# Projections of q and k and the kv tails as matmuls on half the rows, two at a time

## The chip, the cores and the metric

The kernel runs on one core of a Trainium2 chip. The metric is the device time of one execution in microseconds (us), as the median of several runs. A separate execution is recorded by the hardware profiler; its views are called the profile or the trace here. The engines are named as the profile names them: PE (TensorE, matmuls; PEld its weight loads), ACT (ScalarE), DVE (VectorE), POOL (GpSimd) and SP (SyncE, which only issues DMAs here).

## What is computed

Attention with a feature map, then a two-layer network with ELU on its output:

```python
# q, k, v: (8, 8, 576, 64) = batch, heads, rows, head_dim;  w_phi: (64, 128)
def phi(x):
    proj = np.einsum('bhsd,df->bhsf', x, w_phi)
    proj = proj - np.max(np.abs(proj), axis=-1, keepdims=True)
    return np.concatenate([np.exp(proj), np.exp(-proj)], axis=-1)
q_p, k_p = phi(q), phi(k)
kv  = np.einsum('bhsf,bhsd->bhfd', k_p, v)
z   = np.sum(k_p, axis=2)
num = np.einsum('bhsf,bhfd->bhsd', q_p, kv)
den = np.einsum('bhsf,bhf->bhs', q_p, z)[..., None] + 1e-06
x   = (num / den) as (batch * rows, heads * head_dim) = (4608, 512)
h   = x @ w_in                      # w_in (512, 2048)
g   = np.where(h > 0, h, np.exp(np.minimum(h, 0)) - 1)
out = g @ w_out                     # w_out (2048, 512), float32 (4608, 512)
```

## The kernel before

**Work.** The attention is done in 16 quads of four heads each (`plan_quad`, two quads per batch). A head has 576 rows: 512 in the main part and a tail of 64. The tails of two heads share 128 partitions. k and q come in as bf16 and are transposed, the first six quads on PE, the later ones by DMA from SP, into `kT` and `qT`, tiles of 128 partitions: two 64-wide row blocks lie one above the other, on partitions 0 to 63 and 64 to 127. The network (the MoE part of the names) is done in 9 chunks of 512 rows: one per batch from the main parts and one from all tails. A chunk has 16 steps of four matmuls (`mm1`, L975, into banks called `ph`), an exponential on ACT (L987), a subtraction on POOL (L991) and a maximum on DVE (L998), and then 4 x 4 steps of four matmuls (`mm2`, L1036, into `po`).

**The steps of a quad that the change touches.**

- `project` (L535) multiplies a 128-partition tile of `kT` or `qT`, as the stationary operand, with `w_phi_rhs` of 256 columns. That operand, `w_phi_both`, holds `w_phi` on the upper half of the partitions for the first 128 columns and on the lower half for the other 128, and zeros elsewhere, so that one matmul projects both row blocks, each against a half that is zero. Two such matmuls fill one PSUM bank `pk`; a quad has four such banks and a smaller one for the tails, for k and again for q.
- `reduce` (L546, DVE) takes the largest absolute value of each row from `pk` (`m_k`, `m_q`). For k, two exponentials per bank (L561, ACT; plus and minus sign) write `EK` and `EKt`.
- `features` (L668) projects q a second time with the features on the partitions: `w_phi_both[:, par, :]` is stationary and 512 columns of `qT` stream, one matmul into one bank `pq`. Two exponentials per bank (L691, ACT) write `Eq`; `tail_features` (L679) does the tails.
- `kv` (two steps, s = 0 and 1, each with a bank `pkv`): sixteen matmuls of 128 rows (L737) and then four on 64 rows for the tails (L749), s = 0 on partitions 0 to 63 and s = 1 on 64 to 127. `kv_copy` (L760, ACT or DVE) empties the bank.
- `outputs` (L794, `pn`) multiplies `Eq` with `kv`; `tail_outputs` (L809, `pnt`) does so for the tails, with 64 stationary columns, s = 0 on partitions 0 to 63 of the result and s = 1 on 64 to 127. `weigh` (L829) and `combine` (L835) on DVE, then a division, give `x`, which is transposed for the network.

**Order.** The program is written out in full, with each engine's instructions in a fixed order. That order comes from a planner that runs while the program is built (`Planner.run`): it plays the steps forward with a booked cost per step and engine, gives each free engine the ready step of the lowest rank (`RANKS`, one number per step, written into the file), and keeps account of the eight PSUM banks and of DMA: `MB_PER_US` and `MB_PER_US_OF_ONE` (rates), `LANDING` (time until a transfer is seen), `AHEAD` (how far POOL may issue loads in front). A step takes the banks in its list `new` all at once. Steps of the kind `first` (transposes, `pk`, `pq`) start only while they hold fewer than four banks, six before the network has begun:

```python
if kind == "first":
    if held[kind] >= (4 if moe[0] else 6):
        return False
if kind in ("first", "second"):
    n = held["first"] + held["second"] + len(o.new)
    if n > (6 if moe[0] else 8):
        return False
```

On the chip the engines follow the planned order and wait for semaphores; the booked costs are not used there.

Of the kernel before, what the change touches and what calls it, by code (L numbers as in the profile page):

```python
# [8 lines left out]
FP32 = mybir.dt.float32  # L9
# [25 lines left out]
    "0H2r0f2C0G0A2B0k1C0m0K2s092F0E0R201z082A3nD06f55H0Bn4v2+2eAL6C313+3d2o2x01120v2b"  # L35
    "00251m1c020x1Y1r212gBM2D0T173z2I0F1E0q8M07290uF42X2w3b0C0J3Y0h30262j2z1u472V1Z4P"
    "GR4E0LBl0O0o2u0S1x2q3p5F4-0Z150d0W4C28360n0a3c3I0Y4j6n1F4R9G2Q493q6r4L4W2y1T5B5J"
    "3T321g6I0U840s0r2h0z040w1n110i5s2W4x7l5l0B0-1A2n0+3E3x2J4D3J5+1b194n4h4H4m1B4a10"
    "3w7J8P4VAk51504f5A164s0y5D5q6t5N7Z1G1e3K6X4I401i1Q930j1W3h5G1f591v0X7p5O1R2R3v1s"
    "3r3l6R7s3A0cCh2L5x5e4e2vAY8IAZ23GQ7N4F3gGw7kHlDRAG3t4B433a7mH22dGk4r661w5C8BHg24"  # L40
    "Fd9T561hBb5iHC3QA37IAF2YDS9Z9-Av7+C3KX9jDG5n9zAU7FAACK2ZFZA48rBQ798dBLAN5RA89h9O"
    "5vC7AzCmFk9F4+BZDAJOHzA6BE184S3k5d4N4c1+335T7x0e6D0MCj4k1-695r1a1k5cAl715p6E860V"
    "5-7E6i2P6g6-4M0I570p6x2K6S6W3u0PGl7d5V2l746m7C6o8z7M5m7U3-3o6p7o7Q3y4y3O1D414G3P"
    "1o1S3D3m3V3S6L1l2-3C1X3G4Z1q2i3B680NAS5j8p9r5E5X3e6b6T7fAX5P0D7305606h4Y6KBP7X0t"
    "06Gs7A0g816v8e640QBG7T4QAc2H3H6c7W6l6U8f5Q6P7O726M9d7K3X5k8U5t7b8Y3f8G6N8Z7a6q9a"
    "82887D5z8W6e3N3W1U1J7i2f1I1O7r1M132M1H1L2E1V611t9k6B80899fC57z9KH32aDH8lHb9l8D67"
    "Me5W8754KxB0AfDcJtAH7h34C8AOBaAaF+AT9q9NA2CrOY9i9sF2GT2NHRKeGOAg482tBW5UBB2c8X8g"
    "AJAiOcC6Je6dCYAMK12pPBCAKU5KGrFKG5D5DW9JDqIjCXBwKdDbDXEQH+AQHK9mCPGXJ6IIJr9IJa6+"
    "70379M143i4z8t3L4w1y9L1jCa4XETHx7P7v03EVCG7L0lDCC98iBCD61p8aCkAwBg4K7jCz4639DK7B"
    "Bf1P9oDB8SBX6J9ULK9t0b5M7nGcA77S8A837u9D4iB1AKBcBH784JBoDF759x4O91588V4oAC984A2T"  # L50
    "3R8oAP429B4g8v8j766u8wBeHWCd539e92Ee5a9b9YCW6z4pE3JE6AB9K3Fw7q5uCNAxA5B5EqEBBSFI"
    "EXBr5I8-A9275h7V3U3Z5fB+ELDP4lF7BYCSCE355Z4bKyCV8y96CHAtEk8JDjBqC07Y907HCn957G5g"
    "855Y3j8c458hHeCc6G4TD3BA4UGJM48u8O9w2mC1CBJ1ENCoJb2OMSD1GzDNFn9PHBAjLxDTA1FrEvFy"
    "Jd2kFO94JcDyDUHOH8FvFP5yMEJAGiGU5oAnGqGEHGAeFTB6JxAqGmGMH7BDOiEfKT9yDOFcH1DlEKGb"
    "Bk9vDiG3HcDQPQOsBUG6I79QNiGZIJNcMOEwCyHVEHPxQ9JRG2IELTHLOxOBIM447t1K7g8x1ND97eAy"
    "9VCpEOEZFCARCQ7yCJ8KArB3BF9pBN9nBdCFBKAoDZAB628nE-D-DE8N22FM97EWDdBVCqFGEPDu6Y65"
    "Ct9gDYCxD+CwBIF8E2BsFpEFEa9X63HFBy9cAIDVDw5H9ECl5w7wCs4tEmBj8mSBFQ4qJ59HB-DJBpEu"
    "Au8F9SAD3MEME9BREcCME5B4D2G-BhGhHU7-D4BtFlIwESC2HYHj8s8C6FG43F6yDLD7E7EEE+BxG1CL"
    "Cu5LKwDzCiG0Kj9WE6B7E47RCRF-L8Fu8L6aE0I3F6AmDxAEH51dC-6QIQ6O4uJ79R778bFb4d8TAbA0"
    "6wEd9uJQAWAVGWLuKVEsLmJTH4DDPSC+LLD8H9FWDsFLCeHPJ8EzFtMHI8A+HfGvQ8K+GPIxS4FoNeIC"  # L60
    "VnF1LvONTLJ9F9EjS6BODmMyK2FVDeGGVwAsDkIZS2QaO0LhTRAhFiHiJMKkI+QtJVU5RfM2QkReEbK5"
    "HtK7JpJYJLLQInUNGKRBQJ6j8QGB522SGCElFAKAFqEyEGLPCUHrSjBvHyIrCCCg6HIWNMRXQDISC4BJ"
    "ECK4KlGFMUIGRoIVFxKpIPIkHvMFKbHaHDI6L5NlIFQEI1LyJuITNGHqIbPNIXGLI0M9LqFEDtKGCvDp"
    "CbIv6VJgM78kIf2U8+JXQBEDJfNaKJKFILIyJnFFDIKmMz7cMACIMmN1IuNLMdO7CfOpBzM-HQEIL7L4"
    "L0R7SWBT9+HZN0MRLtNXLlK-MDEYNZFmF0P4JNPIIADMIOJ4N6IaLiHNIqPPHsLdMWJBCZJjLkLoN9Ep"
    "DhJkGSEr3s99MV8q8EJP6sNvHh9AObJJ6kHXJqP9LXMqFsLwLGApMIN7SsJGJZDrV+EtFhIDTTEnGgM6"
    "SAAdFUEoW2JDLeLnQ-IzMgHmTbWyDvJyMLEiPHNFKaQpP-OUS3EgNrNTQ5J-GjKPP+K0GIKcUuWkDoDg"
    "Q6JKFgOrW9UIN+LJVBNWGNV5ToRRRaL-UtV4QHPjKqSJUaUCTFUPO9OJUUY6Tp8R5bEx2GKvHoIoFzJm"
    "HJGtMtRHEUIULBSIA-IYL1Q2KzGVLUB8PfI-JwMpKhKLLHNPPFPnPCHkLMEhIcMoKiIpOLMYQPKgP5Hw"
    "JlQGIsL2LVJvLFNVLcPDJiQ1IRKSMcL3G9DaIHG8KIMPItMiLOKOPUMQH6PRIgO-FBLNOjMhKQKYLCLz"  # L70
    "INLjIKLZF5LaN2HEJoJWN5I2BiMxLWHACTBuNKHIJ+MwB2Pg6ZKrNNK9NdQMMBHMO+KNN3OoOfOVFYMu"
    "I4PMKuJzEJJSM1LpKKLYNgHnPYPGPzOAO4KtLgNjLDNONIIhQ7OeHSPbJHP6M3NmE1KWKnOkQTIlLrMJ"
    "RKVkNDO1TSQrFJKEMKEAT7MNS8FDGdPhWAV8DnOEPcX4GHNfTmGAFSPWR+HTO2LsWNWsMkSkWWR0ODM+"
    "PvXrFjOOSgPpL+NkVpWnFRQfWeVLGaOmXyVXDfJIVuWhFaNnWMUqOKMrTzVdImVUVIRZVaX2VFVeUAPa"
    "WRWLUsW5WpXtUxV3VGYKUlBmJ2LRGoG+GDKCOGQRKHM8KfLEGnK6IiGYJCH-PtL6JFI5PsQIIeLbL9TE"
    "RpSQShNAYESYXvTMYAUFOXNbNpP8MfIdNQQ4SPU2KMMXO6SZXRI9GxPqXmSrOtCOLSKoNROhP7ThNYTG"
    "PuKDQ3Pi8HHdQKMGPkQUQNRQSbK8SqN4SFG7JsO5J3KBKsQsP0RFHpHuQONCRLRnF3LARvVYMjRVSnS-"
    "Q0MnN8NHSOUiRuTJGyR-S5TyGuPKRNQgT+NSJhRIJUP3TeR3RrRzOvOgERWaRxWXWbQVScRcUfS0RlNq"
    "U8QLPdVQSLSlO8QXSeSDMTUkT6PTRhWDPwTvUZSdSuUQQvOaJ0WxFNOPViPXMbT-VmXkGpUKQYWvOwNh"
    "WfY0HHLfTOUMNyOZYUP2RMRkX3WwMMV7WQRYOyUWWHQWTBV0YdX7U9UJVWUoMCNxVlQZGfVOWCQCFXSx"  # L80
    "XTQoNuOlWBPOOqXJVHTcUbXlUSXDTsXaXSY7U3W3XNVNTwYBU0S+XbWgXLYPTAE8PANBM0Y5RwR1KRQF"
    "SoSzRWWESyR6T3NUOSUrLIRDSUR8TYTnRJOnRGRjRqQxOWRmXoPJSRYLQQX-T2QhUGWSXOTqTgNEREMs"
    "QwRORsWPXpSwT1UeUTYJR4RTSmYNUOQiXIXCWIVhWFTVTjTWUVVqTxTuOQVSUHUcUERANJVTY4Y3PoVb"
    "PrUyRdTlUvWKQlW0S1SKSMSXVjXETUX+X9TtOTQST8SNR5SVTfQjVoTkWVU1XsRgTZT9YOU-RCStV2Wc"
    "U6V1TPSfYIV6WTSiSGUzVJSvSCUnW7VASSTdQzVfNoUjR2SaQAORRtQeR9VMPyOHUwSTPZMaWtSHUDTX"
    "Y9PeQmULWOWmXVSpXWP1OFUYYaPVTHSEVyQ+XeW4VxPlMvS9WuXzRPV-WrWiU4N-WJQyUgTNWYX0U7Qb"
    "S7QuXgT4YMW1OCUhW8UmKZOIVzY8O3WUWGXwOdRyYkRUX8OMYnWlNwX5TiTaXfYFTDXZWZXdXUYDYXXc"
    "VVVKX6XGUXXuXYXiYfXAYGNtVcW+UBVtYTY2FHV9WqWjURVDYWQqFeTCYVM5T5TQYmWoT0QdYYVsNzUp"
    "YgYHFfVrTrPLPEVCYZXBRbW-W6OuYQWdYRPmMlUdYbY1GeVEYeQnRSRiVvOzMZVPYiXxTKXXXhXKYcXq"
    "YSVRYjVZYlX1XMU+XjXQXnYCTIWzXFXPYhXHVg385S9CCDIBNsQc"  # L90
# [14 lines left out]
class Op:  # L105
    def __init__(self, cost, fn, deps, behind, new, uses, key, load, slot):
        self.cost = cost
        self.fn = fn

        self.deps = [d for d in deps if d is not None]  # L110
        self.behind = [d for d in behind if d is not None]
        self.new = new
        self.uses = uses
        self.key = key
        self.load = load
        self.slot = slot
        self.waits = 0
        self.then = []
        self.engine = None
        self.end = None  # L120
        self.seen = None


class Planner:
# [7 lines left out]
    MB_PER_US = 0.31  # L132
    MB_PER_US_OF_ONE = 0.26
    LANDING = 1.6
    AHEAD = 6.0
# [5 lines left out]
    def op(  # L141
        self, cost, fn, deps=(), behind=(), new=(), uses=(), key=0.0, load=None
    ):
        o = Op(cost, fn, deps, behind, list(new), list(uses), key, load, self.slot)
        for bank in o.new + o.uses:
            bank.users += 1
        self.ops.append(o)
        return o

    def run(self):  # L150
# [58 lines left out]
        while todo:  # L209
            started = False  # L210
            for e in ready:
# [35 lines left out]
                if o.load:  # L247
                    dma = max(dma, o.end) + o.load / self.MB_PER_US
                    o.seen = self.LANDING + max(
                        dma, o.end + o.load / self.MB_PER_US_OF_ONE  # L250
                    )
# [31 lines left out]
def kernel(  # L283
# [11 lines left out]
    P = 128  # L295
# [139 lines left out]
    def plan_quad(i):  # L435
# [38 lines left out]
        for n in range(2):  # L474
# [4 lines left out]
            if i >= DMA_QUAD:  # L479
# [6 lines left out]
                def tail_by_dma(e, n=n, t0=t0):  # L486
# [5 lines left out]
                    {"SP": 1.27}, by_dma, [main, *prior], key=-4.0, load=0.25  # L492
# [3 lines left out]
                    load=0.1,  # L496
# [35 lines left out]
        def project(n, hh, bank):  # L532
            pk = psum(bank, [P, 4, F], FP32, "pk")
            for j in range(2 if hh < 4 else 1):
                nc.tensor.matmul(  # L535
                    pk[:, 2 * j:2 * j + 2, :].rearrange("p a b -> p (a b)"),
                    in_tile(n)[:, 2 * hh + j, :],
                    w_phi_rhs,
                    start=True,
                    stop=True,  # L540
                )

        def reduce(n, hh, bank):
            o = (hh // 2) * NS + (hh % 2) * NT
            m = largest(n)
            nc.vector.tensor_reduce(  # L546
                m[:, o:o + NT] if hh < 4 else m[:, NS - 1::NS],
                bank.tile[:, 0:4 if hh < 4 else 2, :],
# [7 lines left out]
        for hh in range(5):  # L556
            bank = Bank("first")

            def exp_k(e, sg, hh=hh, bank=bank):
                n = 4 if hh < 4 else 2  # L560
                nc.scalar.activation(  # L561
                    EK()[:, hh, sg, :] if hh < 4 else EKt()[:, sg, :],
# [81 lines left out]
        for hh in range(5):  # L644
# [42 lines left out]
            def exp_q(e, sg, c=c, par=par, hh=hh, bank=bank):  # L687
                src = bank.tile
                if hh == 4:
                    src = src.rearrange("p a b -> p (a b)")  # L690
# [506 lines left out]
```

## Time and profile before

| | |
|---|---|
| median of 3 runs | 385.18 us (384.37 to 385.94) |
| the profiled execution's own time | 386.46 us |
| its span, first to last instruction | 384.7 us |
| granted PE clock, mean | 0.998 |
| MATMUL L1036 `po`, records | 550, mean 379 ns |
| MATMUL L975 `ph` from `xT`, records | 495, mean 379 ns |
| MATMUL L535 `pk`, records | 288, means 289 ns (k) and 274 ns (q) |
| MATMUL L668 `pq`, records | 61, mean 379 ns |
| ACT L561 `EK` and L691 `Eq` | 128 each, means 630 and 637 ns |
| DVE L546, k and q | 80 each, means 631 and 630 ns |

The profiled execution is one run, with a time of its own; the median is what is compared. A matmul's duration in the trace runs until its result is out, and the next one starts earlier: how long a row of matmuls takes is read from their starts. Some matmul records are missing. Shapes are given as rows*columns of the stationary operand, then partitions x columns of the streaming one.

### The profile page before, as it was taken

How to read it: one execution, taken by the hardware profiler on the slowest of the kernel's cores; microseconds unless marked ns; L12 is line 12 of the kernel's file. 1: busy time of each engine (PE TensorE's matmuls, PEld its weight loads, DVE VectorE, ACT ScalarE, POOL GpSimd, SP SyncE). 2: the span in 40 equal slices, each digit the busy share in tenths (PEclk: the TensorE clock that was granted, in tenths of full speed). 3: DMA queues.
4: the chain of work that ended last, by engine and by line, in shares of the span. 5: the costliest groups of instructions: out<-in, count | busy, mean ns of one | idle time of the engine just before them, and what ended most of it. 6: DMA issues, size and time to landing. Idle time of an engine off the chain costs nothing.

```text
span 384.7 us, 8031 instructions
## 1 busy us (share of the span) xinstructions
PE 360.1 (94%) x2932; PEld 201.9 (52%) x2978; DVE 265.1 (69%) x560; ACT 266.5 (69%) x576; POOL 245.9 (64%) x356
## 2 busy tenths in 40 slices
PE   3787899999999999999999999989999999999994
PEld 2466556655555545556665456545555554444442
DVE  2989799878677777799894679846963861747000
ACT  2999989677798589688687686677697523646111
POOL 9993999996783399279996642564377552737000
PEclk9999999999999999999999999999999999999999
DMA  8999997689913966954958014781022014000223
GB/s 110 227 203 231 174 166 82 179 107 135 212 33 71 223 130 122 212 117 67 151 121 208 30 38 107 108 225 33 21 56 65 2 41 105 3 28 0 83 61 76
DMA packets 82008, 41.95 MB, mean 109 GB/s; under 512 B 50320, under 2 KB 76048, under 8 KB 81968
## 3 DMA queue, kind: packets, MB, share of 16 engines
q0 software_dynamic: 28992, 14.82, 29.7%
q1 hardware_dynamic: 52976, 26.62, 29.2%
q8 instruction: 23, 0.38, 0.4%
q14 instruction: 17, 0.14, 0.1%
HBM read 36.77 MB, written 9.44 MB: 120 GB/s over the span
## 4 chain that ended last, share of the span: by engine, by line
PE 77%; DMA 7%; ACT 5%; DVE 5%; issue 2%; SPq 1%; POOL 1%; POOLq 0%; ACTq 0%
PE po L1036 30%; PE ph L975 28%; PE pk L535 6%; PE pkv L737 3%; PE pn L794 3%; PE pq L668 2%; ACT EK L561 2%; ACT Eq L691 2%; DMA q_b<-in_q_dram 2%; DMA qT<-q_b 2%; DMA xT<-x 2%; PE pkv L749 1%; DVE tot L829 1%; DMA k_b<-in_k_dram 1%; DMA kT<-k_b 1%
## 5 line engine op out<-in xcount | busy, mean ns | idle before, releaser
L1036 PE MATMUL po<-w_out_sb,gT 128*128 128x512 bf16 x550 | 132.6, 379 | 1.7 <-issue 0.5
L991 POOL TENSOR_SCALAR u_sb<-e_sb 128x512 bf16<-128x512 f32 x144 | 88.0, 619 | 65.1 <-ACT e_sb L987 58.7
L998 DVE SCALAR_TENSOR_TENSOR gT<-u_sb,ph 128x512 bf16<-128x512 bf16 x144 | 95.5, 684 | 42.8 <-POOL u_sb L991 42.4
L975 PE MATMUL ph<-xT,w_in_sb 128*128 128x512 bf16 x495 | 117.1, 379 | 2.4 <-DMA xT<-x 1.6
L987 ACT ACTIVATE e_sb<-ph 128x512 f32<-128x512 f32 x144 | 86.0, 612 | 40.8 <-PE ph L975 37.9
L975 PEld LDWEIGHTS <-w_in_sb 128*128 128x128 bf16 x576 | 55.1, 98 | 61.2 <-issue 2.4
L1036 PEld LDWEIGHTS <-gT 128*128 128x128 bf16 x576 | 54.5, 98 | 55.7
L691 ACT ACTIVATE Eq<-pq 128x512 bf16<-128x512 f32 x128 | 73.0, 637 | 10.0 <-PE pq L668 10.0
L561 ACT ACTIVATE EK<-pk 128x512 bf16<-128x512 f32 x128 | 72.3, 630 | 10.4 <-PE pk L535 10.0
L621 POOL TENSOR_TENSOR vs<-v_b,em 128x512 bf16<-128x512 f32 (+1 forms) x96 | 77.7, 839 | 0.9 <-DMA v_b<-in_v_dram 0.8
L546 DVE TENSOR_REDUCE m_k<-pk 128x4 f32<-128x512 f32 (+1 forms) x80 | 49.2, 631 | 12.0 <-PE pk L535 8.5
L546 DVE TENSOR_REDUCE m_q<-pk 128x4 f32<-128x512 f32 (+1 forms) x80 | 48.7, 630 | 7.4 <-PE pk L535 7.3
L1059 ACT COPY o_sb<-po 128x512 f32<-128x512 f32 x26 | 15.7, 602 | 37.7 <-PE po L1036 36.0
L872 POOL TENSOR_TENSOR x<-tot,rec 128x576 bf16<-128x576 f32 x28 | 31.8, 1154 | 8.6 <-DVE rec L868 8.6
L829 DVE TENSOR_TENSOR tot<-pn,w 128x260 f32<-128x260 f32 x64 | 26.1, 424 | 11.7 <-PE pn L794 11.6
L535 PE MATMUL pk<-w_phi_both,qT 128*128 128x256 bf16 x144 | 26.3, 274 | 2.9 <-DVE m_k L546 1.0
L535 PE MATMUL pk<-w_phi_both,kT 128*128 128x256 bf16 x144 | 27.2, 289 | 1.6 <-ACT EKt L561 0.9
L794 PEld LDWEIGHTS <-Eq 128*128 128x128 bf16 x512 | 21.8, 97 | 8.8 <-issue 0.9
L835 DVE TENSOR_TENSOR tot<-tot,pn 128x260 f32<-128x260 f32 x64 | 25.8, 419 | 0.5
L794 PE MATMUL pn<-kv,Eq 128*128 128x65 bf16 x512 | 24.1, 194 | 0.5 <-ACT kv L760 0.4
L668 PE MATMUL pq<-qT,w_phi_both 128*128 128x512 bf16 x61 | 21.8, 379 | 1.4 <-DVE m_k L546 0.7
L612 POOL CAST vs<-em 128x36 bf16<-128x36 f32 x16 | 5.7, 353 | 27.2 <-ACT em L598 17.3
(66 smaller groups left out, 292.7 us busy)
## 6 DMA issues: line engine op xcount, KB each, us to landing
out_dram<-o_sb SPq DMA_DIRECT2D x32, 256.0 KB, 2.4
v_b<-in_v_dram SPq DMA_DIRECT2D x7, 1024.0 KB, 7.5
k_b<-in_k_dram POOLq DMA_DIRECT2D x7, 512.0 KB, 7.1
q_b<-in_q_dram POOLq DMA_DIRECT2D x7, 512.0 KB, 7.0
w_in_sb<-in_moe_w_in_dram POOLq DMA_DIRECT2D x8, 256.0 KB, 8.0
w_out_sb<-in_moe_w_out_dram POOLq DMA_DIRECT2D x4, 512.0 KB, 11.8
v_b<-in_v_dram POOLq DMA_DIRECT2D x2, 512.0 KB, 6.8
out_dram<-o_sb SPq DMA_DIRECT2D x8, 128.0 KB, 2.3
```

What stands on the lines that cost most here:

```text
L535: nc.tensor.matmul(pk[:, 2 * j:2 * j + 2, :].rearrange("p a b -> p (a b)"), in_tile(n)[:, 2 * hh + j, :], w_phi_rhs, start=True, stop=True,)
L546: nc.vector.tensor_reduce(m[:, o:o + NT] if hh < 4 else m[:, NS - 1::NS], bank.tile[:, 0:4 if hh < 4 else 2, :], axis=AX.X, op=ALU.max, ap ...
L561: nc.scalar.activation(EK()[:, hh, sg, :] if hh < 4 else EKt()[:, sg, :], bank.tile[:, 0:n, :].rearrange("p a b -> p (a b)"), ACT.Exp, sca ...
L621: nc.gpsimd.tensor_tensor(st["vs"][:, sg, r, 0:D], kqv[b, 2][:, o:o + n * D].rearrange("p (n d) -> p n d", d=D), st["em"][:, sg, r, None]. ...
L691: nc.scalar.activation(Eq()[:, par, c, sg, :] if hh < 4 else Eqt()[:, sg, :], src, ACT.Exp, scale=1.0 - 2.0 * sg,)
L794: nc.tensor.matmul(pt[:, t, :], st["Eq"][:, par, c, sg, o:o + P], st["kv"][:, s, c, sg, :], start=True, stop=True,)
L872: (nc.vector if e == "DVE" else nc.gpsimd).tensor_tensor(tile("x", work, [P, NS, 2, D], BF16)[:, :, c, :], tot[:, r, 0:D], st["rec"][:, r, ...
L975: nc.tensor.matmul(ph, w_in_sb[:, ct, jt * P:(jt + 1) * P], xTs[ch][:, ct, :] if ch < B else xT_tail[:, ct // 2, :, ct % 2, :], start=(ct ...
L987: nc.scalar.activation(t["e"], bank.tile, ACT.Exp)
L991: nc.gpsimd.tensor_scalar(t["u"], t["e"], -1.0, 1.0, op0=ALU.add, op1=ALU.mult)
L998: nc.vector.scalar_tensor_tensor(gTs[ch][:, jt, :], t["u"], 0.0, bank.tile, op0=ALU.min, op1=ALU.max)
L1036: nc.tensor.matmul(bank.tile, gTs[ch][:, jt, tt * P:(tt + 1) * P], w_out_sb[:, jt, :], start=(jt == 0), stop=(jt == N_JT - 1),)
```

## The change

`project` works on one column group c of the quad (0, 1, and 2 for the tails) instead of one bank. For c = 0 and 1 it takes two banks and issues eight matmuls of 64 rows and 128 streaming columns, alternating between the lower and the upper half of the partitions, each half into its own bank. `features` likewise takes two banks and issues two matmuls of 64 rows and 512 columns. The zero halves of `w_phi_both` are no longer read there. `EK` and the maxima are laid out accordingly: bank `par` holds the even or odd row blocks. The tail parts of both `kv` steps become a step of their own, `kv_tails`, behind both, with the two halves alternating; both copies of kv wait for it. `tail_outputs` alternates its two halves too. The planner gets other DMA figures, a second figure (`alone`) for a transfer's time by itself, other booked costs for these steps, and a new list of ranks; with it the order of all engines' instructions is new. The main matmuls, exponentials, reductions, loads and stores are otherwise the same in number and size.

```diff
 RANKS = (
-...
+...
 )
-    MB_PER_US = 0.31
+    MB_PER_US = 0.37
     MB_PER_US_OF_ONE = 0.26
-    LANDING = 1.6
-    AHEAD = 6.0
+    LANDING = 3.2
+    AHEAD = 11.0
...
-                    dma = max(dma, o.end) + o.load / self.MB_PER_US
-                    o.seen = self.LANDING + max(
-                        dma, o.end + o.load / self.MB_PER_US_OF_ONE
-                    )
+                    took = o.load / self.MB_PER_US
+                    o.seen = max(o.end + o.alone, dma + took + self.LANDING)
+                    dma = max(dma, o.end) + took
...
-        def project(n, hh, bank):
-            pk = psum(bank, [P, 4, F], FP32, "pk")
-            for j in range(2 if hh < 4 else 1):
+        def project(n, c, pair):
+            pk = [psum(bank, [P, 4, F], FP32, f"pk{par}") for par, bank in enumerate(pair)]
+            if c == 2:
                 nc.tensor.matmul(
-                    pk[:, 2 * j:2 * j + 2, :].rearrange("p a b -> p (a b)"),
-                    in_tile(n)[:, 2 * hh + j, :],
+                    pk[0][:, 0:2, :].rearrange("p a b -> p (a b)"),
+                    in_tile(n)[:, 8, :],
                     w_phi_rhs,
                     start=True,
                     stop=True,
                 )
+                return
+            for j in range(4):
+                for par in range(2):
+                    r = slice(par * D, (par + 1) * D)
+                    nc.tensor.matmul(
+                        pk[par][:, j, :],
+                        in_tile(n)[r, 4 * c + j, :],
+                        w_phi_both[r, par, :],
+                        start=True,
+                        stop=True,
+                    )
...
-            def features(e, c=c, par=par, bank=bank):
-                pq = psum(bank, [P, 4 * P], FP32, "pq")
-                nc.tensor.matmul(
-                    pq,
-                    w_phi_both[:, par, :],
-                    st["qT"][:, 4 * c:4 * c + 4, :].rearrange("p a b -> p (a b)"),
-                    start=True,
-                    stop=True,
-                )
+            def features(e, c=c, pair=pair):
+                for par in range(2):
+                    r = slice(par * D, (par + 1) * D)
+                    nc.tensor.matmul(
+                        psum(pair[par], [P, 4 * P], FP32, f"pq{par}"),
+                        w_phi_both[r, par, :],
+                        st["qT"][r, 4 * c:4 * c + 4, :].rearrange("p a b -> p (a b)"),
+                        start=True,
+                        stop=True,
+                    )
...
             o = add(
-                {"PE": 0.22 if hh < 4 else 0.11},
-                features if hh < 4 else tail_features,
-                [moved[1][0 if hh < 4 else 1], *old("out")],
-                new=[bank],
+                {"PE": 0.28 if c < 2 else 0.11},
+                features if c < 2 else tail_features,
+                [moved[1][0 if c < 2 else 1], *old("out")],
+                new=pair,
...
-                r = slice(s * TAIL, (s + 1) * TAIL)
-                for c in range(2):
-                    for sg in range(2):
+        def kv_tails(e):
+            for c in range(2):
+                for sg in range(2):
+                    for s in range(2):
+                        r = slice(s * TAIL, (s + 1) * TAIL)
                         nc.tensor.matmul(
-                            pkv[:, c, sg, :],
+                            kv_banks[s].tile[:, c, sg, :],
                             st["EKt"][r, sg, c * F:(c + 1) * F],
                             st["vs"][r, sg, c * NS + 8, :],
                             start=False,
...
+        ops["kv"].append(
+            add(
+                {"PE": 0.25},
+                kv_tails,
+                behind=ops["kv"],
+                uses=kv_banks,
+                key=second + 0.22,
+            )
+        )
...
             def tail_outputs(e, pair=pair):
                 pt = psum(pair[0], [P, 2, 2, D1], FP32, "pnt")
-                for s in range(2):
-                    r = slice(s * TAIL, (s + 1) * TAIL)
-                    for sg in range(2):
-                        for c in range(2):
+                for sg in range(2):
+                    for c in range(2):
+                        for s in range(2):
+                            r = slice(s * TAIL, (s + 1) * TAIL)
```

## The prediction

> **What bounds the kernel now.** I read the page's busy table, the slices and the chain of waits first.
>
> ```profile
> PE 360.1 (94%) x2932; PEld 201.9 (52%) x2978; DVE 265.1 (69%) x560; ACT 266.5 (69%) x576; POOL 245.9 (64%) x356
> PE   3787899999999999999999999989999999999994
> PE 77%; DMA 7%; ACT 5%; DVE 5%; issue 2%; SPq 1%; POOL 1%; POOLq 0%; ACTq 0%
> ```
>
> PE is busy for 360.1 of 384.7 us, and 77% of the chain that ended last is PE. But 94% is an average, so I asked for the busy times by stretch.
>
> ```profile
> 20.00:30.00 10.00, 8.62 (x139) 6.26 (x138) 8.81 (x23) 10.00 (x25) 10.00 (x16) 1.00 1.25 209
> 30.00:40.00 10.00, 7.15 (x110) 5.43 (x107) 9.93 (x27) 9.74 (x23) 3.40 (x5) 1.00 1.13 224
> 40.00:50.00 10.00, 8.80 (x94) 5.17 (x96) 7.96 (x18) 9.94 (x21) 9.15 (x14) 1.00 1.16 171
> 60.00:80.00 20.00, 19.79 (x209) 12.83 (x211) 18.79 (x44) 15.95 (x39) 19.17 (x28) 1.00 0.66 122
> 180.00:200.00 20.00, 19.74 (x229) 12.55 (x231) 18.52 (x43) 15.30 (x38) 19.61 (x28) 1.00 0.90 135
> 200.00:220.00 20.00, 19.89 (x149) 10.38 (x149) 12.12 (x26) 14.48 (x32) 13.44 (x20) 1.00 0.49 125
> ```
>
> The columns are stretch, length, then PE, PEld, DVE, ACT and POOL busy. Up to about 50 us ACT (fourth) is full and PE isn't: a shorter matmul is worth nothing there. From 60 us to the end PE is full and the others mostly have room, though DVE and POOL have only 0.4 to 1.5 us in 20 left in some stretches. What PE waits for from 60 to 360 us:
>
> ```profile
> PE ph L975 <- DMA xT<-x: 1.6, 1, 1.6
> PE pk L535 <- DMA qT<-q_b: 0.9, 1, 0.9
> PE po L1036 <- issue: 0.5, 3, 0.2
> PE pkv L737 <- POOL vs L621: 0.3, 1, 0.3
> ```
>
> That is 3.3 us in 300. So in this stage the time is the sum of the PE instructions, and the change is costed as PE time. How much projection work lies there is counted by shape, from 60 to 310 us (later there is no attention):
>
> ```profile
> L737 PE MATMUL pkv<-vs,EK 128*128 128x65 bf16 x416 | 17.7, 194 | 0.3 <-POOL vs L621 0.3
> L749 PE MATMUL pkv<-vs,EKt 64*128 64x65 bf16 x104 | 7.6, 193 | 0.0
> ```
>
> A quad has 32 full kv matmuls and 8 tails; 416/32 = 104/8 = 13, so 13 of 16 quads are in the stage where PE sets the time. The L749 rows are already matmuls on 64 rows, and the order of time shows their price:
>
> ```profile
> 203.11 0.38 PE L668 MATMUL pq<-qT,w_phi_both 128*128 128x512 bf16 x1
> 203.33 0.27 PE L535 MATMUL pk<-w_phi_both,kT 128*128 128x256 bf16 x1
> 203.44 0.67 PE L737 MATMUL pkv<-vs,EK 128*128 128x65 bf16 x16
> 204.04 0.29 PE L749 MATMUL pkv<-vs,EKt 64*128 64x65 bf16 x4
> 204.26 0.39 PE L535 MATMUL pk<-w_phi_both,kT 128*128 128x256 bf16 x2
> ...
> 192.81 0.33 PE L809 MATMUL pnt<-kv,Eqt 128*64 128x65 bf16 x8
> 193.07 1.04 PE L1036 MATMUL po<-w_out_sb,gT 128*128 128x512 bf16 x4
> ```
>
> Durations (second column) hold the latency of the last matmul, so I go by starts. A 512-column matmul starts 0.216 us before the next (0.42 ns a column), a 256-column one 0.109. The sixteen L737 start at 203.44; their last starts 0.19 (its own duration) before 203.44 + 0.67, at 203.92, so they are 0.032 apart. The next start, the first 64-row one, is 204.04: 0.12 later, not 0.03. The last of the four tails starts at 204.04 + 0.29 - 0.19 = 204.14, and the next full one at 204.26, again 0.12 later. The single starts of the trace give 126 ns into the 64-row form (against 31) and 122 ns out of it (against 29), and 309 against 216 from a 512-column matmul into L809. **Every passage between a full and a half form costs 0.093 us, so one stretch in the half form costs 0.186.**
>
> The Trainium skill, "TensorEngine Tiling (Array Packing)", section Tiling Modes, speaks against the change here: changing the tiling mode drains the engine. It gives no time; a sum that left the drain out would gain 13 x 6 x 0.186 = 14.5 us more than mine.
>
> **Projections of k and q (L535).** Removed per quad: 16 matmuls of 256 columns, two to a bank, 16 x 0.109 = 1.74 us. Added: 4 stretches of 8 matmuls of 64 rows and 128 columns. 128 columns are 128 x 0.42 = 0.054 us of streaming, 0.056 by the transposes' starts in this trace. Whether two on different row halves overlap, no row of before shows: L749 uses one half at a time. The bounds are 0.056 a pair (full overlap) and 0.112 (none). The nearest row is L809, eight matmuls on two column halves: from first start to the next full matmul 0.26 us, of which 0.093 is the passage. One after the other they would stream 8 x 0.027 = 0.22, and with the passage 0.31; so the halves did overlap in part, although all of one half were issued before the other. I take overlap, and bound the pair by the loading of weights: the four L749 starts are 35 ns apart, the full ones 32, so two weight loads and matmuls need about 0.064. A stretch is 4 x 0.064 + 0.186 = 0.44, against 0.436 removed: **0.0 us per quad** (full overlap -0.13, none 4 x 0.198 = +0.79).
>
> "TensorE: Matmul & The Clock Gate", Part 3, says that such matmuls run together, starting about 4 ns apart. By it the pair would be 0.060 and the stretch 0.43; no run here shows that yet.
>
> **Features of q (L668).** Two matmuls of 512 columns, 0.432, become a pair on the two halves: 0.216 + 0.186, plus a weight load of 0.03 that waits for nothing: 0.41 to 0.43. Two per quad: **-0.03** (none overlapping: 2 x 0.186 = +0.37).
>
> **Tails of kv (L749).** Removed: two stretches of 4, each 4 x 0.033 + 0.186 = 0.32, together 0.64. Added: one stretch of 8 in pairs: between 4 x 0.033 + 0.186 = 0.32 and 8 x 0.033 + 0.186 = 0.45. **-0.25** (-0.19 to -0.32). The new step waits for both kv stretches, and both copies of kv for it: the copy of s=0 starts about 0.5 us later (16 x 0.032). Behind it are the pn matmuls (L794). They waited for ACT's copy of kv once, 0.4 us, in the whole trace; other matmuls of the MoE stand between, so nothing is charged.
>
> **Tail outputs (L809).** Same eight, halves alternating. Streaming can fall from 0.26 - 0.093 = 0.17 to 8 x 0.0135 (half of 0.027) = 0.11: **-0.03** (0 to -0.06).
>
> **Stretches that fall together.** Two pairs in a row share the passages and save 0.186. From 50 us on, the trace has 93 stretches of L535 and L668 for some 13 quads, about 7 per quad for its 12 such banks: mostly one or two banks at a time, as the banks come free. A pair op takes two banks, so I expect few meetings: 0.75 per quad, **-0.14** (0 to -0.56, three per quad).
>
> **Banks taken by twos.** A pair op now waits until two banks are free. In the trace of before no projection from 60 us on waited for a bank. If a third of the 78 pair ops there waited one exponential (L691, 0.637 us) it would cost 17 us, if none 0. I take 0, because the planner keeps its order by banks and the PE queue holds MoE matmuls in between, but the upper side of the range has it.
>
> **Order and planner.** The ranks, the DMA rates and AHEAD change no instruction, only what stands where. SP's and POOL's queues hold the same loads, transposes and stores, though POOL may issue further ahead. A new wait could cost as much as the longest in this trace, 5.8 us (the first k_b load), and the best it could gain is the 3.3 us of waits above plus some of the first 60 us. I take 0. The planner books 0.28 for a pair step that I put at 0.41 to 0.44, so PE runs later than its plan and the others earlier: that hides waits rather than adding some. What ACT, DVE and POOL do is the same in number and size, apart from bank and stride.
>
> **Sum.** Per quad 0.0 - 0.03 - 0.25 - 0.03 - 0.14 = -0.45; 13 quads give -5.9 us, about -6. The first three quads give nothing, as ACT is full there. The profiled execution took 386.46 us (span 384.7), 1.3 above the median of 385.18; taken off the span it is 378.7, off the median 379.2.
>
> **Rivals.**
> *The halves don't overlap.* Then per quad +0.79 + 0.37 - 0.19 - 0.14 = +0.83, x 13 = +10.8: 396 us, slower. The place is every pair op. It decides from a pair of 0.064 + 0.45/16 = 0.092 us on. For it: no row shows two row halves together; against it: L809.
> *Waits for two banks, or a worse order.* PE full in the profile of before, with 3.3 us of waits, can hardly wait less; 4 to 17 us of new waits against a gain of 6 give 383 to 396. For it: DVE and POOL have no room at 60 to 80 and 180 to 200 us. About 390.
> *Absorbed.* The saved 0.45 per quad goes into waits for POOL and DVE in just those stretches: 385.
> *More than I think.* Full overlap (-0.13), tails -0.32 and three meetings per quad: -1.1 per quad, 371 us; with an order that removes waits it would be 369.
>
> **How the numbers follow.** A difference of 0.5%, 1.9 us, is about what a measurement of this kernel can tell from no change. My forecast (375 to 383) gets 0.40, more than I think 0.12, absorbed 0.15, the halves in series 0.13, the waits 0.20. Faster 0.52, same 0.15, slower 0.33. The likeliest case's own range is 375 to 383. The range of 8 in 10 leaves out the ends of the two outer cases: 371 to 394.
>
> **What would show it.** In the profile after: 64*128 matmuls of 128 columns at the lines of project, with starts alternating by a few ns and about 0.06 per pair; 0.12 at each end of a stretch, more after 512 columns (0.309); L749's successor in one stretch of eight; PE busy near 354 us and still full from 60 us. Wrong: a pair over 0.092 us; PE waits above 6 us after 60; pn waiting for kv's copy; pair ops standing three or four together.

## The result and the profile after

| | before | after |
|---|---|---|
| median | 385.5 us (384.37 to 385.94, 4 runs) | 386.46 us (386.25 to 386.66, 4 runs) |
| ratio after / before | | 1.0029, 95% interval 1.0006 to 1.0053 |
| profiled execution: own time, span | 386.46, 384.7 us | 386.37, 384.6 us |
| mean granted PE clock there | 0.998 | 0.978 |

The changed kernel takes 0.3% longer, within the half per cent called no change. The forecast of 379.2 us was wrong, though the range held the time. Ratios, here and below, leave out executions more than 1.5% above the fastest of the same kernel (one in experiment 8, two in experiment 11); medians are of all. Yet PE has become shorter, as forecast. The page of the changed kernel has the busy times and counts of the engines, PE's 40 slices, the granted clock in tenths, and the shares of the chain of waits:

```profile
PE 353.5 (92%) x3186; PEld 185.7 (48%) x3234; DVE 268.0 (70%) x564; ACT 263.7 (69%) x572; POOL 245.9 (64%) x356
PE   2788578999999999999899999999999999999995
PEclk9988769999999999999999999999999999999999
PE 75%; DMA 10%; POOL 6%; DVE 4%; issue 3%; SPq 1%; ACT 1%; POOLq 0%; ACTq 0%
```

PE is busy 6.6 us less (353.5; "near 354" was expected) and the span is the same. What left PE's work came back as idle time in the fifth slice (38 to 48 us), and the slices 3 to 6 have a lowered clock. The chain has 10% DMA instead of 7%, and POOL 6% instead of 1%. The busy times by stretch, after, in the columns of before:

```profile
20.00:30.00 10.00, 7.91 (x130) 5.92 (x125) 8.55 (x22) 9.16 (x24) 9.40 (x14) 0.83 1.25 197
30.00:40.00 10.00, 8.89 (x125) 5.86 (x124) 9.86 (x23) 10.00 (x25) 8.05 (x13) 0.83 1.13 232
40.00:50.00 10.00, 3.37 (x44) 1.88 (x43) 8.56 (x18) 9.44 (x24) 7.04 (x8) 0.69 1.35 203
60.00:80.00 20.00, 19.16 (x172) 10.28 (x175) 17.22 (x35) 14.39 (x32) 13.54 (x20) 1.00 0.42 70
180.00:200.00 20.00, 18.21 (x150) 8.85 (x148) 14.86 (x31) 12.29 (x28) 13.88 (x21) 1.00 0.85 146
200.00:220.00 20.00, 19.58 (x205) 10.19 (x203) 15.15 (x36) 14.95 (x33) 9.54 (x14) 1.00 0.52 117
```

From 40 to 50 us PE works 3.37 us, where it worked 8.80. Later it is nearly as full as before (busy for 298.2 us from 60 to 365 us, against 299.8). What PE waited for from 60 to 360 us:

```profile
PE ph L1022 <- DVE gT L1045: 2.3, 2, 1.7
PE po L1083 <- issue: 1.3, 8, 0.2
PE pkv L767 <- POOL vs L645: 1.0, 1, 1.0
PE pk L558 <- DVE gT L1045: 0.4, 1, 0.4
```

So the stage that the forecast costed has no more waits to speak of (5 us against 3.3, below the 6 that I had set), and fewer matmul microseconds. The loss lies ahead of it. In the order of time on PE, after:

```profile
45.23 0.40 PE L767 MATMUL pkv<-vs,EK 128*128 128x65 bf16 x4
50.21 1.70 PE L767 MATMUL pkv<-vs,EK 128*128 128x65 bf16 x28 [4.58 <-POOL vs L645]
```

A kv product stands 4.58 us for its scaled v (L645, POOL), in the midst of its 32 matmuls. The other 28 then take 1.70 us: (1.70 - 0.19) / 27 = 0.056 apart instead of 0.032, by a clock of about half. The v that POOL scales late is a load in the chain of waits of after (start, length):

```profile
24.98 17.89 DMA v_b<-in_v_dram
```

In before the v load issued at 27.13 landed in 10.2 us. What such a stall costs is read from how much work is done at 60 us, where PE's full stage begins. The attention is equally far in both kernels (34 `EK` exponentials before and 32 after; 32 `Eq` and 96 `pn` matmuls in both). The network isn't. The weight loads of the first layer begun by 60 us are, before:

```profile
L975 PEld LDWEIGHTS <-w_in_sb x48: 95/98/100, 41.2 to 59.7; 128*128 128x128 bf16 x48
```

and after:

```profile
L1022 PEld LDWEIGHTS <-w_in_sb x16: 96/98/101, 54.6 to 59.0; 128*128 128x128 bf16 x16
```

**32 network matmuls of 0.216 us, 6.9 us of PE work, were done in the first 60 us before and remain to be done after.** The stall is only a part of it. A step of the network's first layer needs x of both quads of a batch, and in after DVE finishes it later. The two instructions that write x of quad 1 are, on DVE before:

```profile
37.90 1.43 DVE L872 TENSOR_TENSOR x<-tot,rec 128x576 bf16<-128x576 f32 x2
```

and after:

```profile
46.01 2.62 DVE L919 TENSOR_TENSOR x<-tot,rec 128x576 bf16<-128x576 f32 x2
```

So x is complete at 48.6 us instead of 39.3, and the first network matmul starts at 54.6 instead of 41.4. For most of the stall there was no network work yet that PE could have done.

The last matmul ends at nearly the same time all the same, so from 60 us on PE must have become some 7 us shorter. I summed it: each matmul at the usual gap to the next start for its kind and the kind behind it, the rest, and what a lowered clock adds, counted as waiting. These sums are good to about 1 us.

| from the first start after 60 us to the last, us | elapsed | work | waiting |
|---|---|---|---|
| before | 319.4 | 314.7 | 4.6 |
| after | 318.7 | 313.7, with 6.9 more to do | 5.0 |

At equal work to do the matmul time fell by some 8 us. The theory then: the half-row forms bring even more than was costed, and the new order spends it before 60 us. The rivals: the half clock is what spends it, or the late DMA, or the forms don't bring it.

### The profile page after: what moved, and what is told of

Read it like the earlier page. It is cut to its first block, busy times and chain, and to the rows that moved or that the text cites. A ratio compares the mean times of both kernels' runs of the same rounds, so it can differ in the third digit from the quotient of the medians.

```text
span 384.6 us, 8543 instructions
## 1 busy us (share of the span) xinstructions
PE 353.5 (92%) x3186; PEld 185.7 (48%) x3234; DVE 268.0 (70%) x564; ACT 263.7 (69%) x572; POOL 245.9 (64%) x356
## 4 chain that ended last, share of the span: by engine, by line
PE 75%; DMA 10%; POOL 6%; DVE 4%; issue 3%; SPq 1%; ACT 1%; POOLq 0%; ACTq 0%
PE po L1083 31%; PE ph L1022 27%; DMA v_b<-in_v_dram 5%; PE pk L558 4%; DMA qT<-q_b 4%; PE pn L841 3%; PE pkv L767 3%; POOL vs L645 2%; PE pq L693 2%; PE tr L517 1%; DVE gT L1045 1%; DVE m_q L569 1%; DMA k_b<-in_k_dram 1%; POOL q_b L396 1%; PE pk L547 1%
## 5 line engine op out<-in xcount | busy, mean ns | idle before, releaser
L1022 PE MATMUL ph<-xT,w_in_sb 128*128 128x512 bf16 x493 | 119.6, 379 | 3.4 <-DVE gT L1045 2.3
L1022 PEld LDWEIGHTS <-w_in_sb 128*128 128x128 bf16 x576 | 53.2, 98 | 61.3 <-issue 3.6
L645 POOL TENSOR_TENSOR vs<-v_b,em 128x512 bf16<-128x512 f32 (+1 forms) x96 | 77.5, 833 | 5.0 <-DMA v_b<-in_v_dram 4.9
L1083 PEld LDWEIGHTS <-gT 128*128 128x128 bf16 x576 | 51.8, 98 | 56.5 <-issue 3.0
L593 ACT ACTIVATE EK<-pk 128x512 bf16<-128x512 f32 x128 | 70.5, 624 | 7.7 <-PE pk L558 7.5
L727 ACT ACTIVATE Eq<-pq 128x512 bf16<-128x512 f32 x128 | 70.0, 636 | 7.6 <-PE pq L693 7.5
L919 POOL TENSOR_TENSOR x<-tot,rec 128x576 bf16<-128x576 f32 x28 | 31.9, 1153 | 13.2 <-DVE rec L915 11.3
L767 PE MATMUL pkv<-vs,EK 128*128 128x65 bf16 x512 | 22.8, 202 | 6.4 <-POOL vs L645 6.2
L767 PEld LDWEIGHTS <-EK 128*128 128x128 bf16 x512 | 20.5, 103 | 11.8 <-issue 7.0
L841 PE MATMUL pn<-kv,Eq 128*128 128x65 bf16 x512 | 24.9, 195 | 0.9 <-ACT EKt L593 0.4
L693 PE MATMUL pq<-qT,w_phi_both 64*128 64x512 bf16 x64 | 14.3, 413 | 1.2 <-DVE tot L876 0.8
```

What stands on the lines that cost most here:

```text
L593: nc.scalar.activation(EK()[:, 2 * c + par, sg, :] if c < 2 else EKt()[:, sg, :], bank.tile[:, 0:n, :].rearrange("p a b -> p (a b)"), ACT.Exp,
L645: nc.gpsimd.tensor_tensor(st["vs"][:, sg, r, 0:D], kqv[b, 2][:, o:o + n * D].rearrange("p (n d) -> p n d", d=D), st["em"][:, sg, r, None]. ...
L727: nc.scalar.activation(Eq()[:, par, c, sg, :] if c < 2 else Eqt()[:, sg, :], src, ACT.Exp, scale=1.0 - 2.0 * sg,)
L767: nc.tensor.matmul(pkv[:, c, sg, :], st["EK"][:, 2 * c + par, sg, o:o + F], st["vs"][:, sg, c * NS + s * NT + t, :], start=first, stop=Fal ...
L841: nc.tensor.matmul(pt[:, t, :], st["Eq"][:, par, c, sg, o:o + P], st["kv"][:, s, c, sg, :], start=True, stop=True,)
L919: (nc.vector if e == "DVE" else nc.gpsimd).tensor_tensor(tile("x", work, [P, NS, 2, D], BF16)[:, :, c, :], tot[:, r, 0:D], st["rec"][:, r, ...
```

## Experiments

Each ran against the kernel before on the same chip; the kernel before had medians of 385.1 to 386.3 us there, with 15 to 20 runs a time.

**1. The new order with full rows.** It undoes the half-row projections and features alone. Order, planner, tails and banks stay as in after:

```diff
-                        in_tile(n)[r, 4 * c + j, :],
-                        w_phi_both[r, par, :],
+                        in_tile(n)[:, 4 * c + j, :],
+                        w_phi_both[:, par, :],
...
-                        w_phi_both[r, par, :],
-                        st["qT"][r, 4 * c:4 * c + 4, :].rearrange("p a b -> p (a b)"),
+                        w_phi_both[:, par, :],
+                        st["qT"][:, 4 * c:4 * c + 4, :].rearrange("p a b -> p (a b)"),
```

> The changed kernel with the same order of every engine, but the projections and features of q and k on all 128 rows again (eight 128x128 matmuls, two 128x512); the kv tails stay paired. Theory A (the half-row forms save PE time, the new order loses it in the first 60 us): by the starts in the changed kernel's trace a projection stretch costs 0.415 us and would cost 0.448, a feature stretch 0.417 against 0.435; 4 and 2 per quad, 13 quads: 2.2 us slower than the changed kernel, about 388.7. Rival B (half-row matmuls make the clock gate see too little work, and the half clock between 23 and 54 us is theirs): the clock stays whole and the time falls, to 381 to 384.

Measured: 388.67 us (388.01 to 390.99), ratio 1.0095 (1.0063 to 1.0127), 2.2 us above after. The work from 60 us on is 319.1 us against 313.7: by this sum half rows save 5 us there, of which the spans of the profiled executions show 3.8 and the medians 2.2. Its first 60 us have the same fault as after's. Network weight loads of this kernel by 60 us:

```profile
L1020 PEld LDWEIGHTS <-w_in_sb x16: 96/98/101, 55.5 to 59.9; 128*128 128x128 bf16 x16
```

Its clock was whole from 20 to 40 us, where after had 0.83, and still it has done 16. x of quad 1 is complete at 47.9 us there, and kv stands 4.88 us for POOL. So the start is lost by the order, not by the half-row form, and not by the half clock that after has between 23 and 37 us. From 48.4 to 55.2 us the clock is half here too, about the stall and behind it; what that stretch adds isn't separated from the order.

**2. The loads of w_out behind the scaling of v**, to bring v sooner (edit in the planner's output, order of the other steps unchanged):

```diff
+        w_out, v_scaled, held_back = self.ops[23:27], self.ops[312], []
...
-                o.fn(e)
+                if o in w_out:
+                    held_back.append(o)
+                else:
+                    o.fn(e)
+                if o is v_scaled:
+                    for x in held_back:
+                        x.fn("POOL")
```

> The changed kernel with one thing moved: POOL issues the four loads of w_out behind the first scaling of v that waited for v, instead of around the load of v of batch 1. Theory A (this load, 17.9 us in landing, makes the stall of 4.6 us at 45 to 50 us and the half clock around it): v lands in under 10 us, the stall is gone, the clock is whole for longer, 380 to 382.5. Rival (ACT or something else sets the pace up to 60 us anyway): the wait moves and the time stays at 385 or more.

Measured: 392.52 us (390.79 to 393.74), ratio 1.0179 (1.0147 to 1.0212). v landed in 12.9 us instead of 17.9, the stall at 45 us shrank from 4.58 to 2.75, and a new one came up in the waits of this kernel's PE before 64 us, that of quad 3's kv product:

```profile
PE pkv L774 <- DVE gT L1052: 4.3, 1, 4.3
```

**3. The loads of k and q of the batches 2 and 3 behind it too:**

```diff
+        late = self.ops[539:543] + self.ops[23:27] + self.ops[801:805]
+        v_scaled, held_back, flushed = self.ops[313], [], False
...
```

> The changed kernel; POOL issues the loads of w_out and of k and q for batches 2 and 3 only behind the last scaling of v of quad 2. Theory (POOL's queue in the new order, loads in front of and between the scalings of v, makes the stalls of PE at 45 to 50 us): v lands in 8 to 12 us, kv of quad 2 doesn't wait for POOL, more than 30 network matmuls are done by 60 us, 380 to 384. Rival (the later loads are then late themselves, or PE's own order is at fault, with only four network steps ahead of kv of quad 3): the wait moves to transposes or kv of quad 3, 386 to 392.

Measured: 392.35 us (391.46 to 395.01), ratio 1.0157 (1.012 to 1.0193). The stall of quad 2 is gone, and quad 3's is longer. Order of time on PE in this kernel:

```profile
55.50 1.03 PE L1031 MATMUL ph<-xT,w_in_sb 128*128 128x512 bf16 x4
64.91 0.38 PE L776 MATMUL pkv<-vs,EK 128*128 128x65 bf16 x4 [8.38 <-DVE gT L1054]
```

The network's weight loads by 60 us are 16 in both runs again; in this one:

```profile
L1031 PEld LDWEIGHTS <-w_in_sb x16: 95/98/101, 51.5 to 55.9; 128*128 128x128 bf16 x16
```

Both runs, which also make other loads later, speak against the late v of quad 2 as the cause by itself: without its stall the network still begins at 51.5 us, 10 us behind before, since x of quad 1 is complete only at 48.9. What stays is the fixed order: in the changed order the kv product of quad 3 stands behind only four network steps (16 matmuls), in before behind sixteen, where it ran at 69.6 us. PE goes through its instructions in order, so whatever delays this one product (POOL's scaling, a load, or in these two runs, by the profile, a network step on DVE) holds up the network matmuls behind it.

**4 and 5. Does PE time set the time?** The kernel before, without its 128 kv tail matmuls (`no_tails`), and with each of them three times (`tails_thrice`):

```diff
-                        nc.tensor.matmul(
-                            pkv[:, c, sg, :],
-                            st["EKt"][r, sg, c * F:(c + 1) * F],
-                            st["vs"][r, sg, c * NS + 8, :],
...
+                for turn in range(3):
```

> The kernel before, in its own order, without the kv tails' 128 matmuls (their part of the result is left out): the two stretches in a quad, 0.64 us of PE time, are gone; 13 quads from 60 us on, 8.3 us. Theory A (from 60 us on PE is full, so PE time is time): about 377. Theory B (the order of before is made so that other chains - transposes by DMA, POOL, ACT - end just ahead of PE; relief of PE turns into waits): 382 to 385.5, with PE waits after 60 us up from 4.6 to 9 us or more.

> The kernel before, in its own order, with each stretch of kv tails issued three times over (the tails count threefold in the result): 16 more 64-row matmuls in a quad at 0.033 us, 0.53 us, 13 quads: 6.9 us more PE time, 8.5 with the first three quads. Both theories: slower. Theory A (symmetric): 392 to 394. Theory B (one-sided: PE is on the path when it gets longer, other chains when it gets shorter): also 391 to 394, so that the pair with the kernel without tails decides.

Measured: 382.89 us (381.17 to 385.71), ratio 0.9917 (0.9879 to 0.9956), without; 394.25 us (392.36 to 396.82), ratio 1.0223 (1.0175 to 1.027), with three. Taking away PE work priced at 8.3 us (some 7 by the sum from 60 us on) gave 2.4 us; by the interval it can be 1.7 to 4.7. Adding work priced at 7 to 8.5 us (some 6 by that sum) cost 9.0. Without the tails, the waiting after 60 us rose from 4.6 to 8.8 us. Among the waits that are new or longer in the kernel without tails are some for DMA, ACT and DVE:

```profile
PE ph L964 <- DMA xT<-x: 2.0, 1, 2.0
PE pn L783 <- ACT kv L749: 0.5, 1, 0.5
PE pk L535 <- DVE gT L987: 0.5, 2, 0.3
```

In the order of before, then, PE can be made longer at full price, but shorter at about a third of it. I read this so that transposes by DMA, copies on ACT and steps on DVE are hardly behind PE.

**6 and 7. The tails alone (of kv and of the outputs) in the order of before**, for all quads (`tails_alone`), and from quad 3 on (`tails_late`):

```diff
+        def kv_tails(e):
+            for c in range(2):
+                for sg in range(2):
+                    for s in range(2):
+                        ... one matmul into kv_banks[s] ...
...
+        TAIL_FROM = 3
```

> The kernel before with the kv tails as one stretch of four pairs and the tail outputs alternating, nothing else; ranks from the plan of before. The two stretches of tails cost 0.64 us in a quad, the one costs 0.32 by the changed kernel's starts: 13 x 0.33 = 4.3 us. Theory A (PE time saved from 60 us on is time saved): 381.2. Rival (it is absorbed by other engines): 384 to 386.

> The kernel before; from quad 3 on the kv tails are one stretch of four pairs and the tail outputs alternate; quads 0 to 2 and the plan of the first 60 us are those of before. Theory (the forms save PE time as computed, and what is lost is lost in the first 60 us, where latency and order count): the 0.32 us in each of 13 quads come out less some new waits: 381 to 383, against 387.5 where quads 0 to 2 had the new tails too. Rival (the order of before is fitted to its PE times, and any saving turns into waits later): 384.5 to 387.

Measured: 387.48 us (385.96 to 388.58), ratio 1.0049 (1.0031 to 1.0068); and 386.63 (385.62 to 387.15), ratio 1.0003 (0.9982 to 1.0025). In both the matmul work from 60 us on fell by 3 to 4 us and the waiting rose, to 7.1 and 8.4 us. One wait in `tails_late` shows a second price of waiting. Its stretches, in the same columns:

```profile
98.00:102.00 4.00, 1.91 (x34) 1.28 (x31) 1.62 (x3) 1.45 (x4) 4.00 (x7) 1.00 1.39 239
102.00:106.00 4.00, 4.00 (x20) 1.99 (x19) 2.66 (x6) 1.55 (x5) 1.88 (x3) 0.57 0.65 68
106.00:110.00 4.00, 4.00 (x21) 1.96 (x20) 2.00 (x4) 2.97 (x8) 1.24 (x2) 1.00 0.17 66
```

PE stands from 98.8 us (1.9 us at a stretch, for a DVE step), and then the granted clock is half from 102.1 to 105.5, which costs some 1.7 us more.

**8 and 9. All forms in the order of before**, in all quads with the old DMA figures and the costs that I had put (`pairs_old_order`), and from quad 3 on (`pairs_late`, which alone has the last two lines):

```diff
-                {"PE": 0.28 if c < 2 else 0.11},
+                {"PE": 0.42 if c < 2 else 0.11},
...
+        PAIR_FROM = 3
+        TAIL_FROM = 3
```

> All of the change's matmul forms, with the planner's DMA figures of before and ranks taken from the times at which the plan of before started each step (a pair of banks at the mean of its two steps), 0.42 us booked for a pair stretch and 0.33 for the kv tails. Theory A: the PE work saved (0.45 us in each of 13 quads) comes out at the end: 379.5, between 377 and 382.5, with a whole clock. Rival B (the half rows cost the clock): half clock before 60 us and 385 or more. Rival C (taking banks by twos makes PE wait in any order): PE waits of over 6 us after 60 us, 383 to 388.

> All of the change's matmul forms from quad 3 on, quads 0 to 2 as before, the planner's DMA figures of before, ranks from the plan of before (a pair at the mean of its two steps), 0.42 us booked for a pair stretch. Theory (first 60 us): about as many network matmuls before 60 us as before (48), waits of PE after 60 us up to 8 us, 380 to 385. Rival (banks by twos make PE wait wherever the order was not made for them): waits of 12 us and more after 60 us as in the kernel with pairs throughout in the old order (16.6 us), 388 to 394.

Measured: 398.34 us (394.79 to 400.75), ratio 1.0308 (1.0256 to 1.0359); and 390.24 (388.15 to 391.63), ratio 1.0088 (1.0054 to 1.0122). The waiting after 60 us is 16.6 and 14.0 us, against 4.6 in before, and 36 and 40 network matmuls are done by 60 us instead of 48. The largest single item of the waiting is that for the transposes of x:

```profile
PE ph L1216 <- DMA xT<-x: 4.2, 2, 2.9
```

(`pairs_late`). The work is 4.5 us less than in before there. The change of form in the order of before is a loss, of 3.1% in all quads and of 0.9% from quad 3 on.

**10. Ranks searched for the measured costs** (all forms from quad 3 on, the planner's own time as the goal):

```diff
 RANKS = (
-...
+...
 )
```

> All of the change's forms from quad 3 on, as in the kernel with late pairs (390.2), with ranks searched for them by the planner, on measured costs (0.42 us a pair stretch) and for two landing times of DMA; the plan of the first 50 us is that of before. By the plan 372.6 us against 378.2 unsearched and 375.1 for the kernel before. Theory (what the forms save is lost to an order that wasn't made for them): PE waits after 60 us fall from 14 to 5 to 8 us, 381 to 385. Rival (banks by twos cost the waits in any order): 388 and more.

Measured: 390.63 us (387.77 to 393.56), ratio 1.011 (1.0047 to 1.0173). The plan went from 378.2 to 372.6 us; on the chip the work from 60 us on is the least of all (305.8 us) and the waiting the most (19.3, some 5 of it from three stretches of half clock). What the planner gains isn't what the chip gains: the plan of before says 375.1 and that of after 360.9 us, and both have spans of 384.6 to 384.7.

**11 and 12. The start of before and the rest of after.** Forms, ranks and DMA figures of before until 60 us, and then those of after (`early_before_late_after`); the same with a pair step booked at 0.42 in place of 0.28 (`early_before_measured`):

```diff
+    SWITCH = 60
+    MB_PER_US = 0.31, 0.37
+    LANDING = 1.6, 3.2
+    AHEAD = 6.0, 11.0
...
+    PAIR_FROM = 4
+    TAIL_FROM = 4
```

> The first 60 us in the plan and the forms of the kernel before (quads 0 to 3), then the forms and the ranks of the changed kernel with its DMA figures and its booked 0.28 us. Theory (the changed kernel saves about 8 us of PE work from 60 us on, at the same waits, and loses 6.9 of it because 32 network matmuls fewer are done by 60 us): 48 network matmuls by 60 us, waits of 5 to 7 us after, 378 to 381. Rival (the ranks of the changed kernel fit only its own start; with another they bring waits, as in the other mixed orders): waits of 10 us and more after 60 us, 385 to 389.

> The same with the measured costs booked for the late steps (0.42 us a pair stretch, 0.33 the kv tails) instead of 0.28 and 0.25. Theory: an order planned with true PE times waits no more than the one planned with 0.28; within 2 us of it. Rival (the booked 0.28 leaves other engines slack, as PE runs late against its plan): 2 to 5 us slower than the one with 0.28.

Measured: 384.39 us (381.86 to 387.88), ratio 0.9948 (0.9926 to 0.997); and 388.54 (386.2 to 389.49), ratio 1.0067 (1.0047 to 1.0087). The first is half a per cent faster than the kernel before, at the edge of what can be told from no change, and by its median it is also below after, which did not run beside it. Its network weight loads by 60 us are 48 again:

```profile
L1228 PEld LDWEIGHTS <-w_in_sb x48: 95/98/147, 41.1 to 60.0; 128*128 128x128 bf16 x48
```

Its work from 60 us on is 309.1 us and its waiting 6.2; the profiled execution has a span of 380.6 us, 4.0 below after's. By the medians only 2.1 of the 6.9 us came back (2.5 without its two slowest runs). The second has the same work (309.3) but 13.2 us of waiting, some 3 of it from two stretches of half clock after 60 us, which the first doesn't have, and 3.2 in one wait:

```profile
PE ph L1228 <- DVE tot L1079: 3.2, 1, 3.2
```

So with these ranks the booked 0.28, which is below the measured 0.42, is worth 4 us. That PE then runs behind its plan, and finds what it needs, is how I read it; the waits (6.2 against 13.2) agree with it. That the ranks fit only the cost with which they came isn't excluded: no run has other ranks with 0.28.

## Why the prediction was wrong

**The forms: right.** All starts are read in the order of time on PE, after:

```profile
86.23 0.40 PE L558 MATMUL pk<-w_phi_both,kT 64*128 64x128 bf16 x8
86.56 1.04 PE L1083 MATMUL po<-w_out_sb,gT 128*128 128x512 bf16 x4
...
95.22 0.30 PE L793 MATMUL pkv<-vs,EKt 64*128 64x65 bf16 x8
95.35 0.38 PE L693 MATMUL pq<-qT,w_phi_both 64*128 64x512 bf16 x2
95.66 1.04 PE L1083 MATMUL po<-w_out_sb,gT 128*128 128x512 bf16 x3
```

- *Passages.* 0.093 was put; single starts give 0.095 into the half form (311 against 216 ns) and about 0.09 out of it (the next full matmul 0.148 after the last start instead of 0.056).
- *Projections.* The halves overlap: the two of a pair start 3 to 4 ns apart and the next pair 53 ns later, 0.056 where 0.064 was put and 0.092 would have decided the other way. From first start to the next full matmul it is 86.56 - 86.23 = 0.33, with 0.095 in front 0.415 to 0.42 against 0.436 removed: -0.08 per quad, 0.0 forecast.
- *Features.* 95.66 - 95.35 = 0.31 and 0.1 in front: -0.03 per quad, as forecast.
- *Tails.* 0.095 + 7 x 0.015 + 0.122 = 0.32 for what took 0.64: -0.32, where -0.25 was taken and -0.32 was the bound.
- *Tail outputs.* Their starts are 17 ns apart instead of 19: -0.01, not -0.03.
- *Stretches that meet.* In the lines above the features begin 0.13 after the tails without a passage between. From 60 us on there are 99 steps in the half form (49 projections, 24 features, 13 kv tails, 13 tail outputs) in 84 stretches: 15 meetings, 1.15 per quad of 13, where 0.75 was taken: -0.21, not -0.14.

The 13 quads of the sum were read from the kv product; projections and features run ahead of it, and of them only some 12 quads lie behind 60 us. Together the pieces give 49 x 0.02 + 24 x 0.015 + 13 x 0.32 + 13 x 0.01 + 15 x 0.186 = 8.4 us, about 0.65 per quad of 13 instead of 0.45. The ledger, at equal work to do, says 8. The groups from 60 to 312 us carry the counts of features and tails (48 are 24 steps, 104 are 13 quads):

```profile
L693 PE MATMUL pq<-qT,w_phi_both 64*128 64x512 bf16 x48 | 8.9, 383 | 0.0
L793 PE MATMUL pkv<-vs,EKt 64*128 64x65 bf16 x104 | 3.9, 193 | 0.0
```

The Trainium skill has the overlap in "TensorE: Matmul & The Clock Gate", Part 3: tiles of one pack start some 4 ns apart. The 3 to 4 ns here agree.

**The step that failed: "Order and planner. ... I take 0", with "The first three quads give nothing".** I had costed the first 60 us as if they could only stay as they were, since ACT is full there. But PE uses the gaps of that stage for the network, 48 matmuls of it in before, and a new order can lose them: after makes x of quad 1 9.3 us later, and its PE order has only 16 of them by 60 us. That is +6.9 us, and with the 8 us won from 60 us on the sum is near zero (the span fell by 0.1 us, the medians rose by 1). The text named a worst case, one new wait of 5.8 us; a wait of that kind came, 4.58 us, and the sum went without it. It is a part of the loss only: run 3 hasn't got it and still has 16. The signs of being right that the text named came about as named; none of them looks at the first 60 us.

**A premise that was too simple: "in this stage the time is the sum of the PE instructions".** 3.3 us of waits in 300 show that PE is seldom late. They don't show by how much the others are early. Runs 4 and 5 measure that: about a third of what is taken away comes out, and all of what is added. At a third of the forecast 5.9 us, the forms in the order of before would have been worth about 2 us, and runs 8 and 9 gave less than nothing. What the order of after does better is that its waiting stays at 5.0 us although the work is shorter.

**The rivals.** *The halves don't overlap:* refuted. *Waits for two banks, or a worse order:* this is what happened, in its second half, and before 60 us, where I hadn't looked for it. In runs 8 to 10 it is 14 to 19 us of waiting after 60 us, 9 to 15 more than in before, as its text had it (4 to 17); whether banks taken by twos or the shifted order make them is not separated. *Absorbed:* `tails_late` is a plain case of it, 3 to 4 us less work and the time unchanged. *More than I think:* true in part of the terms, -0.65 per quad where it had -1.1, and false of the time. Of the signs of error that I had named, pn waiting for kv's copy is not to be seen in the waits of after, and three steps stand together in one stretch only.

**Open.** What makes v land 17.9 us after its issue is not taken apart: runs 2 and 3 move other loads and shorten it, with worse results elsewhere. Why run 11 brings back 2.1 us by the medians and not 6.9 is open in part; its profiled execution, with 382.38 us one of its faster ones, brings 4.0. There the work from 60 us on (309.1) is 2.3 us above after's 313.7 less the 6.9, and the waiting 1.2 us above after's. Nor is it settled why after has more half clock than run 1 with the same order (mean clock of all runs 0.972 to 0.987 against 0.982 to 0.991).

## What to carry to other kernels

Price a stretch of half-row matmuls with its two passages, 0.19 us here, and put such stretches together: the passages saved by meetings (0.21) and by making two tail stretches one (0.19) are 0.40 of the 0.65 us won per quad. Before you call an engine's busy time the time, take some work off it and add the same to it in an unchanged order; if the two don't answer alike, other chains stand just behind it. And with a new order, count first how much of the bulk work is done when the full stage begins: 32 matmuls missing at 60 us cost 6.9 us here, and no row of the later stage shows them.

## What the runs showed of the hardware

- A stall of PE can be paid twice. In `tails_late` a wait of 1.9 us was followed by 3.4 us of half clock. The length of the wait alone doesn't decide: waits of 2.0 us in `no_tails` and 2.5 in `tails_thrice` were followed by none. In after the clock is half from 43.7 to 54.0 us, around the wait of 4.58. The stretches of half clock last 3.4 us or a multiple (3.4, 6.8, 10.2); they are 17.1 us in all in after, and none in before from 14.3 us to its last matmul.
- The Trainium skill, "TensorE: Matmul & The Clock Gate", Part 1, gives a window of about 3.4 us for this gate, and half rate after an idle one. The length agrees; the idle time ahead of the half clock in `tails_late` was shorter than a window.
- The passage between full and half rows costs 0.09 to 0.10 us behind long matmuls and short ones: 311 against 216 ns behind 512 columns, 126 against 32 behind 65.
- The same kernel, with PE work priced at 7 to 8.5 us taken off or added, answers with 2.4 us on the one side and 9.0 on the other.
